# Attention and a gated convolution on one core: the w_val weights, xh and xl at other SBUF offsets, and another order of the work

## The chip, the cores and the metric

The kernel runs on one core of a Trainium2 chip. TensorE (PE in the profile, its weight loads PEld), VectorE (DVE), ScalarE (ACT), GpSimd (POOL) and SyncE (SP) each work through their own list of instructions in order and wait for one another by semaphores. SP does no arithmetic here; it issues every DMA. The metric is the time of one execution on the device, in microseconds.

## What is computed

The reference, cut to its core (`log`, `exp` and so on are numpy's):

```python
# q, k, v: (4, 8, 768, 64)
k_sum = k.reshape(B, H, nb, 32, D).max(axis=3)
v_sum = v.reshape(B, H, nb, 32, D).mean(axis=3)
scores_l = where(abs(pos_i - pos_j) < 16, scale * q @ k.T, -1e9)
scores_s = scale * q @ k_sum.T + log(32)
a = softmax(concatenate([scores_l, scores_s]))       # eps 1e-9
x = (a @ concatenate([v, v_sum])).to (4, 768, 512)
gate = sigmoid(causal depthwise convolution of x with conv_w, 5 taps)
out = (gate * (x @ w_val)) @ w_out                   # w_val, w_out: 512 x 512
```

## The kernel before

The work falls into 12 groups g (4 batches times 3 thirds of the sequence, 256 positions each); a group has two units u of four heads. A unit is computed in two halves r of two heads each. Every piece of work has a short name, and the string `ORDER` is a list of these names; a loop at the end of the kernel calls them one after the other. Each engine (and SP's list of DMAs) receives its instructions in exactly this order; nothing reorders them later, and semaphores make consumers wait. The pieces that matter here, with the lines of the kernel before:

- `s` scores on TensorE (L515), `n` the mask and row maximum on VectorE (L531), `e` exp on ScalarE (L544), `r` reciprocal of the row sum on VectorE (L551), `m` normalisation of p on GpSimd (L556), `t` transposes of p on TensorE (L566), `c` their copy to `pts` (L573), `x` the product with v on TensorE (L583).
- `X`, `Y` copies of the product to `xh` (rounded to fp32r) and `xf` (full fp32) on ScalarE (L594, L598), `Z` the rest `xl` = xf - xh on GpSimd (L602), `I`, `T`, `G` the gate: start value, taps on VectorE (L620), tanh.
- `v` the product with w_val on TensorE (L640). `v g.cp.r` makes 12 matmuls that accumulate one 128x256 tile: eight with `xh` as the moving operand (with the high part and the low part of the weights by turns, for four chunks of 128 rows), then four with `xl` and the high part. The stationary operand is a 128x128 block of the tile `wv`. There are 44 such pieces in fp32r, 528 matmuls; group 0 does it in fp32 with the tile `wf` instead.
- `gf`, `gh`, `gl` the gated value, its rounded part and the rest; `o` the product with w_out on TensorE (L676), 12 matmuls of 512 columns with `gh` or `gl` stationary and `wo` moving; `ob` and `O` scale and store.
- `Lk`, `Lq`, `Lv`, `Lu`, `Lwv`, `Lwo` loads; `Lu b.i` fetches a batch's transposed values (tile `vT`) for the block means that `tv` sums on GpSimd (L248, four halvings and a last sum), `vsp` transposes on TensorE and `vsc` copies out; `F g` writes these means into the value tile by four DMAs (L325). `ks` and `kc` make the block maxima of the keys, `vp`, `vc`, `vb`, `vbc` the means of batch 0, `W` warm-up matmuls on zeros, `hal` the convolution's halo.

Tiles lie in SBUF in the order in which the pools are opened, and within a pool in the order of first use. In the kernel before the small constants (pool `csm`: mask, taps, lag, row sums) come first and fill 2432 bytes of a partition from 16512, so that `ident`, `wv`, `wo`, `wf`, `pts`, `gh`, `gl`, `xh` and `xl` all start at a multiple of 512 bytes.

Of the kernel before, what the change touches and what calls it, by code (L numbers as in the profile page):

```python
# [60 lines left out]
r2 n3.1 x0.1 t1.0 Lk1.0 m1.1 Lwv2 ks1.1 I0 Y0 c1.0 T0.0 s4.0 e3.0 s4.1 t1.1 c1.1 x1.0 e3.1 rbwv0
wlwv3 m2.1 m2.0 n4.1 shwv0 n4.0 ks1.0 r3 orwv0 x1.1 t2.1 c2.1 Y1 shwv2 rbwv2 s5.0 s5.1 orwv2
t2.0 T0.1 n5.1 Lv1 Lu1.1 Lk1.3 Lq3 tv1.2 e4.0 m3.0 c2.0 kc1.1 kc1.0 m3.1 Lu1.0 wcwv2 hal1 v0.0.0
F1 e4.1 wcwv1 G0 v0.0.1 t3.1 v0.1.0 n5.0 c3.1 t3.0 Lk1.2 s6.0 s6.1 I1 r4 ks1.3 x2.0 wcwv0 c3.0
e5.0 x2.1 Y2 T1.0 n6.1 ks1.2 n6.0 gf0.0 wlwv2 tv1.1 m4.0 t4.0 v0.1.1 tv1.0 X2 x3.0 c4.0 x3.1
kc1.3 kc1.2 Lwo1 Lu1.3 s7.0 tv1.3 rbwo1 e5.1 m4.1 s7.1 Z2 vsp1 t4.1 X3 Y3 Z3 wlwv0 v1.1.0 T1.1
# [46 lines left out]
def tile_attention_then_gated_conv(  # L113
# [204 lines left out]
    def fill_vs(g):  # L318
# [470 lines left out]
```

## Time and profile before

| | |
|---|---|
| median of 3 runs | 243.63 us (243.48 to 244.19) |
| profiled execution, its own time | 242.4 us |
| its span (first to last instruction) | 239.8 us |
| PE / ACT / DVE / POOL busy, share of the span | 95 / 79 / 76 / 63 % |
[...]

The profiled execution's time is 2.6 us longer than its span (what lies before the first and after the last instruction), and 1.2 us (0.5%) under the median. A matmul's busy time overlaps with that of the next, so the distance between the starts of matmuls, not their durations, tells what they cost.

### The profile page before, as it was taken

How to read it: one execution, taken by the hardware profiler on the slowest of the kernel's cores; microseconds unless marked ns; L12 is line 12 of the kernel's file. 1: busy time of each engine (PE TensorE's matmuls, PEld its weight loads, DVE VectorE, ACT ScalarE, POOL GpSimd, SP SyncE). 2: the span in 40 equal slices, each digit the busy share in tenths (PEclk: the TensorE clock that was granted, in tenths of full speed). 3: DMA queues.
4: the chain of work that ended last, by engine and by line, in shares of the span. 5: the costliest groups of instructions: out<-in, count | busy, mean ns of one | idle time of the engine just before them, and what ended most of it. 6: DMA issues, size and time to landing. Idle time of an engine off the chain costs nothing.

```text
span 239.8 us, 7492 instructions
## 1 busy us (share of the span) xinstructions
PE 227.1 (95%) x2736; PEld 197.6 (82%) x2736; DVE 182.8 (76%) x698; ACT 190.6 (79%) x620; POOL 151.0 (63%) x222
## 2 busy tenths in 40 slices
PE   4778999999999999999989999999999999999993
PEld 1347788899998899898888898898988998899982
DVE  4899999998899979978989689868586565435800
ACT  2589999989999987998997999997896398174322
POOL 4153998971999989678678809994069603822620
PEclk9999999999999999999999999999999999999999
DMA  6999989999388468600693777405506221120022
GB/s 208 378 404 405 405 323 310 391 321 354 72 264 302 147 220 283 228 31 6 189 406 95 256 210 247 160 3 112 187 14 240 62 63 46 44 116 18 0 87 89
DMA packets 19812, 46.14 MB, mean 192 GB/s; under 512 B 2336, under 2 KB 7200, under 8 KB 19776
## 3 DMA queue, kind: packets, MB, share of 16 engines
q1 hardware_dynamic: 19776, 45.68, 55.5%
q8 instruction: 21, 0.34, 0.6%
q14 instruction: 15, 0.12, 0.2%
HBM read 37.21 MB, written 6.29 MB: 181 GB/s over the span
## 4 chain that ended last, share of the span: by engine, by line
PE 68%; DMA 7%; DVE 7%; POOL 6%; ACT 5%; SPq 3%; issue 2%; ACTq 0%; POOLq 0%; DVEq 0%
PE out L676 26%; PE val L640 21%; PE x L583 8%; PE pt L566 7%; PE s L515 6%; DMA k<-in_kT_dram 3%; DMA vT<-in_vT_dram 2%; DMA out_dram<-ob 2%; DVE sn L531 2%; ACT p L544 2%; POOL vT L248 2%; DVE g L620 2%; POOL p L556 2%; POOL xl L602 2%; SPq L325 1%
## 5 line engine op out<-in xcount | busy, mean ns | idle before, releaser
L620 DVE SCALAR_TENSOR_TENSOR g<-xf,cwt,g 128x256 f32<-128x256 f32 x192 | 93.7, 488 | 23.7 <-ACT xf L598 9.1
L544 ACT ACTIVATE p<-sn,nm 128x120 f32<-128x120 f32 x192 | 73.4, 390 | 7.5 <-DVE nm L531 7.5
L556 POOL TENSOR_TENSOR p<-p,ri 128x480 f32<-128x480 f32 x48 | 47.0, 993 | 13.8 <-DVE ri L552 9.8
L640 PE MATMUL val<-xh,wv 128*128 128x256 f32 x352 | 51.9, 290 | 0.0
L640 PEld LDWEIGHTS val<-xh,wv 128*128 128x128 f32 x352 | 44.9, 190 | 0.2
L531 DVE CUSTOM_DVE_ANT_0 sn<-s,mask 128x120 f32<-128x120 f32 x192 | 41.7, 276 | 4.1 <-PE s L515 3.9
L676 PE MATMUL out<-wo,gh 128*128 128x512 f32 (+1 forms) x184 | 44.3, 383 | 0.0
L602 POOL TENSOR_TENSOR xl<-xf,xh 128x512 fp32r<-128x512 f32 x22 | 28.2, 1289 | 25.2 <-ACT xh L594 16.9
L654 POOL TENSOR_TENSOR gl<-gf,gh 128x512 fp32r<-128x512 f32 x22 | 28.1, 1287 | 22.7 <-ACT gh L651 22.7
L676 PEld LDWEIGHTS out<-wo,gh 128*128 128x128 f32 x184 | 32.9, 188 | 6.2 <-issue 0.2
L544 ACT ACTIVATION_READ_ACCUMULATOR p<-sn,nm 128x1 f32 x192 | 37.3, 194 | 0.0
L573 ACT COPY pts<-pt 120x512 f32<-120x512 f32 x48 | 28.0, 583 | 11.6 <-PE pt L566 11.5
L566 PE MATMUL pt<-ident,p 128*120 128x128 f32 x192 | 30.1, 279 | 1.9 <-POOL p L556 1.7
L583 PE MATMUL x<-pts,v 120*64 120x64 f32 x768 | 29.8, 226 | 0.1
L583 PEld LDWEIGHTS x<-pts,v 120*64 120x64 f32 x768 | 26.1, 137 | 4.1 <-issue 1.3
L640 PE MATMUL val<-xl,wv 128*128 128x256 f32 x176 | 28.7, 284 | 0.6 <-POOL xl L602 0.6
L515 PE MATMUL s<-k,q 64*64 64x120 f32 x768 | 26.1, 272 | 2.2 <-POOL xf L456 0.6
L248 POOL TENSOR_TENSOR vT<-vT 128x384 f32<-128x384 f32 (+3 forms) x44 | 25.0, 568 | 5.0 <-DMA vT<-in_vT_dram 2.4
L566 PEld LDWEIGHTS pt<-ident,p 128*120 128x120 f32 x192 | 21.2, 137 | 7.1 <-POOL p L556 2.3
L515 PEld LDWEIGHTS s<-k,q 64*64 64x64 f32 x768 | 20.1, 134 | 7.5 <-POOL k L234 2.2
L640 PEld LDWEIGHTS val<-xl,wv 128*128 128x128 f32 x176 | 24.3, 191 | 1.0 <-POOL xl L602 1.0
L676 PE MATMUL out<-wo,gl 128*128 128x512 f32 (+1 forms) x92 | 23.8, 380 | 0.0
(64 smaller groups left out, 273.1 us busy)
## 6 DMA issues: line engine op xcount, KB each, us to landing
v<-in_vw_dram SPq DMA_DIRECT2D x24, 512.0 KB
k<-in_kT_dram SPq DMA_DIRECT2D x16, 478.0 KB
vT<-in_vT_dram SPq DMA_DIRECT2D x16, 384.0 KB
out_dram<-ob SPq DMA_DIRECT2D x23, 256.0 KB
q<-in_qT_dram SPq DMA_DIRECT2D x11, 512.0 KB
raw_wv<-in_wv_dram SPq DMA_DIRECT2D x4, 512.0 KB
raw_wo<-in_wo_dram SPq DMA_DIRECT2D x4, 512.0 KB
v<-vs SPq DMA_DIRECT2D x36, 48.0 KB
```

What stands on the lines that cost most here:

```text
L248: nc.gpsimd.tensor_tensor(dst, src[:, :, :n], src[:, :, n : 2 * n], ALU.add)
L515: nc.tensor.matmul(sp(u)[64 * e : 64 * e + 64, h, c * KW : c * KW + KW], qt(g)[64 * h : 64 * h + 64, pr, i * QT : i * QT + QT], ktile[b, p ...
L531: nc.vector.tensor_tensor_reduce(sn(u)[:, n, :], sp(u)[:, h, c * KW : c * KW + KW], mask[:, mv, :], -1.0 / math.sqrt(D), 3.0e38, ALU.add, ...
L544: nc.scalar.activation(pr_(u)[:, n, :], sn(u)[:, n, :], AF.Exp, bias=nm(u)[:, n : n + 1], scale=-1.0, accum_out=rs(u)[:, n, 0:1],)
L556: nc.gpsimd.tensor_tensor(pr_(u)[:, w], pr_(u)[:, w], st["ri", u][:, w].unsqueeze(2).broadcast_to([P, TPU, KW]), ALU.mult,)
L566: nc.tensor.transpose(pt[:KW, i, :], pr_(u)[:, TPU * r + i, :], ident)
L583: nc.tensor.matmul(dst, v[:KW, i, c0 : c0 + D], src, start=True, stop=g > 0)
L602: nc.gpsimd.tensor_tensor(xl(g)[:, two(hp), :], xf(g)[:, two(hp), HALO:], xh(g)[:, two(hp), :].bitcast(F32), ALU.subtract,)
L620: nc.vector.scalar_tensor_tensor(gp(u)[:, r], xf(g)[:, pr, o : o + SG], cwt[:, pr, o : o + 1], gp(u)[:, r], ALU.mult, ALU.add,)
L640: nc.tensor.matmul(pp[:, r], w, x, start=(n == 0), stop=(n == len(terms) - 1))
L654: nc.gpsimd.tensor_tensor(gl(g)[:, two(cp), :], grp["gf", g, cp], gh(g)[:, two(cp), :].bitcast(F32), ALU.subtract)
L676: nc.tensor.matmul(pp, x, w, start=(n == 0), stop=(n == len(terms) - 1))
```

## The change

**The layout.** `wv` gets a pool of its own that is opened first, then come small tiles (`ks`, `nm`, `ri`, together 448 bytes), then `xh` and `xl` (pool `px`; the raw w_out words that share their buffers move with them), then small tiles again (`vsT` and one row sum, 448 bytes), then everything else; the constants come last. The starts of the tiles modulo 512 bytes, worked out from the sizes of the tiles:

| tile | before | after |
|---|---|---|
| wv (stationary in `v`) | 0 | 128 |
| xh, xl (moving in `v`) | 0 | 64 |
| wo, gh, gl, wf, gf, ident, pts, v, q | 0 | 0 |
| p, three buffers | 64, 320, 64 | 256, 0, 256 |
| xf, two buffers | 320, 384 | 0, 64 |

All blocks of `wv`, `xh` and `xl` that a matmul reads lie at multiples of 512 bytes from the tile's start, so every one of the 528 matmuls has its operands at these offsets. No instruction is added or removed, and no buffer count changes.

**The order.** `ORDER` is another permutation of the same words; every engine gets the same instructions in another sequence. Two of its lines stand in the diff. Three places:

On TensorE before the first product with v (`x_0`): `pt` are transposes, `vb` those of batch 0's block means, the number after `s`, `x`, `p` is the unit, the two numbers after `pt` unit and half. Before:

```order
L301 MATMUL vb_1_344<-ident_91,vpad_94 128x128 x4
L301 MATMUL vb_0_349<-ident_91,vpad_94 128x128 x4
L295 LDWEIGHTS warm_95
L295 MATMUL warm_out_116<-warm_95 128x512
L295 LDWEIGHTS warm_95
L295 MATMUL warm_out_116<-warm_95 128x512
L515 MATMUL s_3_356<-k_0_2_134,q_1_247 64x120 x8
L515 MATMUL s_3_356<-k_0_3_187,q_1_247 64x120 x8
L583 MATMUL x_0_385<-pts_0_301,v_0_310 64x64
```

and after:

```order
L575 MATMUL pt_0_1_320<-ident_103,p_0_202 120x128 x4
L575 MATMUL pt_1_0_346<-ident_103,p_1_264 120x128 x4
L524 MATMUL s_3_352<-k_0_2_129,q_1_198 64x120 x8
L524 MATMUL s_3_352<-k_0_3_175,q_1_198 64x120 x8
L299 LDWEIGHTS warm_107
L299 MATMUL warm_out_125<-warm_107 128x512
L305 MATMUL vb_1_398<-ident_103,vpad_106 128x128 x4
L305 MATMUL vb_0_405<-ident_103,vpad_106 128x128 x4
L299 LDWEIGHTS warm_107
L299 MATMUL warm_out_125<-warm_107 128x512
L592 MATMUL x_0_431<-pts_0_311,v_0_313 64x64
```

The transposes of unit 1 and the scores of unit 3 now stand ahead of `vb`; before, the scores stood behind it and the first transposes of unit 1 behind `x_0`.

On SP in the middle of the program, where the means of batch 2 (`vs_2`) are written into the value tile of group 6 (`F6`) and the values of batch 3 (`vT_3_...`) are fetched. Before:

```order
L204 DMA vT_3_1_1838<-in_vT_dram 128x768
L691 DMA out_0_dram<-ob_2_1_1766 128x512
L211 DMA v_6_1933<-in_vw_dram 128x1024 x2
L325 DMA v_6_1933<-vs_2_2012 12x2x512 x4
L195 DMA q_8_2071<-in_qT_dram 128x1024
L691 DMA out_0_dram<-ob_1_0_1662 128x512
L204 DMA vT_3_3_2074<-in_vT_dram 128x768
L211 DMA v_7_2082<-in_vw_dram 128x1024 x2
L199 DMA k_3_0_2207<-in_kT_dram 128x956
```

and after:

```order
L199 DMA q_7_1761<-in_qT_dram 128x1024
L208 DMA vT_3_3_1780<-in_vT_dram 128x768
L329 DMA v_5_1581<-vs_1_960 12x2x512 x4
L199 DMA q_8_1832<-in_qT_dram 128x1024
L700 DMA out_0_dram<-ob_2_0_1601 128x512
L203 DMA k_3_2_1835<-in_kT_dram 128x956
L215 DMA v_6_1967<-in_vw_dram 128x1024 x2
L329 DMA v_6_1967<-vs_2_1897 12x2x512 x4
L208 DMA vT_3_0_2189<-in_vT_dram 128x768
L208 DMA vT_3_2_2191<-in_vT_dram 128x768
L700 DMA out_0_dram<-ob_3_0_2180 128x512
```

The load of `vT_3_3` stood behind the four DMAs that wait for `vs_2`; now it stands ahead of them, and those of `vT_3_0` and `vT_3_2` follow them.

On GpSimd between the two halves of unit 10's normalisation (`p_10`; `vT_2_1` and `vT_2_3` are values of batch 2 that `tv` sums, `k_2_...` the block maxima that `kc` writes). Before, from the first half to the second:

```order
L556 TENSOR_TENSOR p_10_1437<-p_10_1437,ri_10_1528 128x480
L248 TENSOR_TENSOR vT_2_1_1325<-vT_2_1_1325 128x24x16
L248 TENSOR_TENSOR vT_2_1_1325<-vT_2_1_1325 128x24x8
L248 TENSOR_TENSOR vT_2_1_1325<-vT_2_1_1325 128x24x4
L248 TENSOR_TENSOR vT_2_1_1325<-vT_2_1_1325 128x24x2
L248 TENSOR_TENSOR vsT_2_1_1597<-vT_2_1_1325 128x24
L234 COPY k_2_2_950<-ks_2_2_1684 128x7x12
L234 COPY k_2_2_950<-ks_2_2_1684 128x6x12
L602 TENSOR_TENSOR xl_4_1751<-xf_4_1544,xh_4_1682 128x512
L234 COPY k_2_3_1515<-ks_2_3_1699 128x7x12
L234 COPY k_2_3_1515<-ks_2_3_1699 128x6x12
L556 TENSOR_TENSOR p_10_1437<-p_10_1437,ri_10_1528 128x480
```

and after, where the first half stands five rows ahead, from the last sum of `vT_2_1` to the second half:

```order
L252 TENSOR_TENSOR vsT_2_1_1698<-vT_2_1_1549 128x24
L463 TENSOR_SCALAR xf_4_1645<-xf_3_1293 128x4x4
L252 TENSOR_TENSOR vT_2_3_1543<-vT_2_3_1543 128x24x16
L252 TENSOR_TENSOR vT_2_3_1543<-vT_2_3_1543 128x24x8
L252 TENSOR_TENSOR vT_2_3_1543<-vT_2_3_1543 128x24x4
L252 TENSOR_TENSOR vT_2_3_1543<-vT_2_3_1543 128x24x2
L252 TENSOR_TENSOR vsT_2_3_1748<-vT_2_3_1543 128x24
L238 COPY k_2_3_1477<-ks_2_3_1692 128x7x12
L238 COPY k_2_3_1477<-ks_2_3_1692 128x6x12
L238 COPY k_2_2_788<-ks_2_2_1613 128x7x12
L238 COPY k_2_2_788<-ks_2_2_1613 128x6x12
L565 TENSOR_TENSOR p_10_1359<-p_10_1359,ri_10_1538 128x480
```

One sum of a value tile, two pairs of copies and one `xl` stood between the two halves; now it is two sums, a halo and two pairs of copies, and both halves of `xl_4` follow behind.

## Rows read from the trace of the kernel before

**Rows 1.** The page: the span, busy times and slices of the whole execution.

```profile
span 239.8 us, 7492 instructions
...
PE 227.1 (95%) x2736; PEld 197.6 (82%) x2736; DVE 182.8 (76%) x698; ACT 190.6 (79%) x620; POOL 151.0 (63%) x222
...
PEclk9999999999999999999999999999999999999999
```

**Rows 2.** Busy time of each engine from 20 to 180 us, columns as headed.

```profile
core 0: us, PE busy (x) PEld busy (x) DVE busy (x) ACT busy (x) POOL busy (x), PEclk, DMA share, GB/s
...
20.00:180.00 160.00, 157.62 (x2146) 140.61 (x2146) 140.34 (x558) 148.57 (x502) 119.16 (x166) 1.00 0.65 218
```

**Rows 3.** The chain that ended last, pieces in time: start us, us, what.

```profile
55.63 7.15 PE out L676 x64
...
158.70 1.43 PE val L640 x12
```

**Rows 4.** Groups of instructions by line, TensorE: busy us, mean ns.

```profile
L640 PE MATMUL val<-xh,wv 128*128 128x256 f32 x352 | 51.9, 290 | 0.0
...
L640 PE MATMUL val<-xl,wv 128*128 128x256 f32 x176 | 28.7, 284 | 0.6 <-POOL xl L602 0.6
```

**Rows 5.** TensorE's timeline, single starts: start us, us, operation.

```profile
194.24 0.52 PE L640 MATMUL val<-xh,wv 128*128 128x256 f32 x3
194.36 0.52 PE L640 MATMUL val<-xh,wv 128*128 128x256 f32 x3
194.49 0.52 PE L640 MATMUL val<-xh,wv 128*128 128x256 f32 x3
...
229.91 0.52 PE L676 MATMUL out<-wo,gh 128*128 128x256 f32 x3
230.02 0.52 PE L676 MATMUL out<-wo,gh 128*128 128x256 f32 x3
```

**Rows 6.** Lines 566 and 620: duration ns min/median/max, first and last start.

```profile
L566 PE MATMUL pt<-ident,p x192: 270/273/326, 14.7 to 211.5; 128*120 128x128 f32 x192
...
L620 DVE SCALAR_TENSOR_TENSOR g<-xf,cwt,g x192: 437/490/494, 24.7 to 225.9; 128x256 f32<-128x256 f32 x192
```

**Rows 7.** Timelines of VectorE and TensorE in the first 21 us, and busy times there.

```profile
4.55 0.95 DVE L220 TENSOR_REDUCE ks<-k 128x24 f32<-128x768 f32 x1
...
18.50 1.09 PE L301 MATMUL vb<-ident,vpad 128*128 128x128 f32 x8 [0.36 <-POOL vpad L284]
...
20.94 0.34 PE L583 MATMUL x<-pts,v 120*64 120x64 f32 x4
...
4.55:18.25 13.70, 11.02 (x124) 5.29 (x122) 12.14 (x56) 8.62 (x43) 4.93 (x22) 1.00 1.03 388
```

**Rows 8.** The chain that ended last, 111 to 127 us.

```profile
111.61 0.59 ACT vs L315
...
116.59 5.71 DMA vT<-in_vT_dram
...
125.19 0.95 POOL p L556
```

**Rows 9.** GpSimd's and TensorE's timeline at unit 10, and TensorE's at 126 us.

```profile
87.49 2.49 POOL L248 TENSOR_TENSOR vT<-vT 128x384 f32<-128x384 f32 x4 [0.94 <-DMA vT<-in_vT_dram]
...
90.24 0.99 POOL L556 TENSOR_TENSOR p<-p,ri 128x480 f32<-128x480 f32 x1
...
94.34 1.29 POOL L602 TENSOR_TENSOR xl<-xf,xh 128x512 fp32r<-128x512 f32 x1
...
95.97 1.93 POOL L556 TENSOR_TENSOR p<-p,ri 128x480 f32<-128x480 f32 x2
...
94.63 0.60 PE L566 MATMUL pt<-ident,p 128*120 128x128 f32 x4
...
98.66 0.65 PE L566 MATMUL pt<-ident,p 128*120 128x128 f32 x4
...
126.19 0.65 PE L566 MATMUL pt<-ident,p 128*120 128x128 f32 x4 [0.89 <-POOL p L556]
```

More of the change, by code (lines that the diff above doesn't have):

```diff
@@ L61 @@
[L61 to L66, printed above, removed]
@@ new lines @@
+s0.0 n0.0 kc0.1 Lk0.3 Lp2 Ln1 W11 s0.1 W12 Lp3 ks0.2 vp3.0 n0.1 Lq1 W13 W14 e0.0 ks0.3 kc0.2 W15
+ez kc0.3 vc3.0 s1.0 W16 e0.1 Ln0 Lc n1.0 W17 s1.1 Lwv3 Ln2 vp1.0 r0 n1.1 e1.0 e1.1 Lwv0 vp1.1
+vp0.0 shc m0.0 hal0 s2.0 t0.0 s2.1 W18 W19 m0.1 r1 vc1.0 m1.0 c0.0 Lv0 rbwv3 Lwv2 t0.1 vp0.1
+n2.1 n2.0 vp2.0 c0.1 vp2.1 rbc e2.0 t1.0 m1.1 s3.0 vc0.0 vc2.0 c1.0 Lwv1 rbwv0 s3.1 vp3.1 vc0.1
+vc2.1 vc1.1 n3.1 vc3.1 shwv3 W20 shwv0 orwv0 orwv3 n3.0 orc vb1 vbc1 vb0 Lu1.1 Lq2 Lv1 vbc0
+Lk1.0 Lk1.1 e2.1 wcwv3 rbwv2 W21 x0.0 x0.1 W22 W23 t1.1 Y0 I0 r2 shwv2 c1.1 wcwv0 orwv2 x1.0
@@ new lines @@
+x1.1 shwv1 rbwv1 s4.0 wcwv2 Y1 s4.1 T0.0 e3.0 orwv1 e3.1 wlwv3 m2.1 m2.0 v0.0.0 t2.0 wlwv0
+v0.0.1 n4.1 T0.1 ks1.0 r3 ks1.1 n4.0 wlwv2 Lu1.2 c2.0 G0 Lk1.2 tv1.1 m3.1 m3.0 t2.1 wcwv1 I1 F1
+v0.1.0 c2.1 T1.0 t3.1 s5.0 s5.1 Lwo1 n5.1 tv1.2 x2.0 e4.0 Lk1.3 c3.1 x2.1 Lq3 e4.1 t3.0 v0.1.1
+kc1.1 kc1.0 n5.0 Lu1.0 Lu1.3 Lv2 Y2 X2 c3.0 x3.0 e5.0 r4 x3.1 m4.1 s6.0 m4.0 t4.0 X3 Lwo3 Lwo0
+T1.1 gf0.0 Y3 s6.1 Lk2.2 F2 Lwo2 Z2 ks1.3 ks1.2 n6.0 Z3 hal1 e5.1 c4.0 G1 r5 wlwv1 kc1.3 m5.0
+tv1.0 v1.1.0 hal2 kc1.2 tv1.3 v1.0.0 gf0.1 n6.1 I2 v1.1.1 t4.1 T2.0 v1.0.1 e6.0 rbwo1 c4.1 T2.1
@@ new lines @@
+t5.0 vsp1 m5.1 s7.0 shwo0 s7.1 x4.0 e6.1 rbwo0 vsc1 x4.1 c5.0 orwo0 G2 gf1.0 t5.1 I3 o0.0.0
+o0.1.0 shwo1 orwo1 X4 Y4 wcwo0 rbwo2 rbwo3 o0.0.1 o0.1.1 x5.0 c5.1 shwo2 n7.0 n7.1 shwo3 Lq4
+e7.0 x5.1 s8.0 s8.1 orwo3 orwo2 e7.1 wcwo3 X5 gh1.0 r6 n8.0 n8.1 Lv3 o0.0.2 o0.1.2 o0.1.3 m6.0
+Z4 m6.1 o0.0.3 Lu2.2 Y5 s9.0 Z5 s9.1 T3.0 r7 T3.1 t6.0 Lk3.3 F3 ob0.1 Lv4 e8.0 ob0.0 c6.0 wcwo2
+G3 gl1.0 Lq6 Lq5 v2.1.0 n9.1 Lk2.1 I4 wcwo1 t6.1 v2.1.1 v2.0.0 wlwo0 m7.1 m7.0 c6.1 t7.1 n9.0
+x6.0 wlwo1 wlwo3 wlwo2 x6.1 s10.0 gf1.1 T4.0 T4.1 s10.1 hal3 gh1.1 gl1.1 Lk2.0 O0.0 Lu2.0 tv2.2
@@ new lines @@
+e8.1 c7.1 t7.0 r8 n10.0 e9.0 G4 v2.0.1 m8.0 O0.1 F4 m8.1 I5 gf2.0 e10.0 e9.1 X6 o1.0 o1.1 Y6
+c7.0 T5.0 T5.1 t8.1 n10.1 s11.0 tv2.0 G5 I6 s11.1 x7.0 r9 x7.1 gf2.1 ks2.1 c8.1 gh2.0 t8.0 ks2.0
+Lk2.3 T6.0 gh2.1 c8.0 T6.1 n11.1 gl2.0 X7 ob1.0 n11.0 gl2.1 o2.0 o2.1 Y7 e10.1 ob1.1 r10 G6
+Lu2.3 I7 m9.0 Lu2.1 O1.0 kc2.1 Z7 Z6 kc2.0 m9.1 m10.1 t9.0 v3.1.0 ob2.1 Lv5 O1.1 Lk3.1 x8.0
+e11.0 ob2.0 c9.0 x8.1 ks2.2 T7.0 T7.1 s12.0 s12.1 t9.1 Y8 e11.1 c9.1 G7 X8 I8 v3.0.0 v3.1.1 r11
+n12.0 ks2.3 n12.1 tv2.1 t10.1 gf3.1 c10.1 e12.0 v3.0.1 x9.0 x9.1 hal4 tv2.3 kc2.3 kc2.2 m10.0
@@ new lines @@
+Lk3.0 Lq7 gf3.0 T8.0 Y9 X9 s13.0 Lu3.3 s13.1 Z8 t10.0 vsp2 e12.1 T8.1 n13.0 r12 n13.1 c10.0
+gh3.0 gh3.1 Z9 F5 Lq8 O2.0 Lk3.2 v4.0.0 G8 I9 m11.0 v4.1.0 T9.0 t11.0 v4.1.1 e13.0 c11.0 vsc2
+gl3.1 m11.1 T9.1 x10.0 e13.1 x10.1 hal5 m12.0 gl3.0 s14.0 s14.1 t11.1 o3.0 c11.1 Lv6 F6 G9 Y10
+X10 I10 tv3.3 m12.1 t12.0 n14.0 n14.1 r13 gf4.1 s15.0 s15.1 x11.0 x11.1 m13.1 c12.0 T10.0 t12.1
+v4.0.1 T10.1 ks3.0 e14.0 Y11 X11 gh4.1 e14.1 gf4.0 c12.1 G10 r14 n15.0 Z11 o3.1 t13.1 kc3.0 Z10
+m13.0 m14.1 gl4.1 m14.0 hal6 I11 v5.1.0 x12.0 x12.1 n15.1 s16.0 e15.0 ob3.0 c13.1 e15.1 Y12
@@ new lines @@
+Lu3.0 Lu3.2 O3.0 s16.1 t13.0 v5.1.1 v5.0.0 tv3.2 T11.0 T11.1 X12 c13.0 G11 I12 t14.1 v5.0.1 r15
+x13.0 x13.1 ks3.1 n16.0 n16.1 gf5.1 Lv7 T12.0 s17.0 gh4.0 e16.0 c14.1 gl4.0 s17.1 t14.0 X13 Y13
+ob3.1 e16.1 o4.0 F7 Z13 m15.0 c14.0 m15.1 kc3.1 o4.1 T12.1 n17.0 G12 r16 n17.1 ks3.2 ks3.3 gf5.0
+I13 e17.0 Lq9 O2.1 T13.0 e17.1 s18.0 ob4.0 s18.1 m16.1 hal7 kc3.3 Z12 x14.0 m16.0 T13.1 x14.1
+t15.0 v6.0.0 c15.0 t15.1 Lu3.1 v6.1.0 c15.1 Y14 X14 t16.1 O4.0 O3.1 Lv8 n18.1 r17 n18.0 v6.0.1
+Z14 kc3.2 G13 I14 T14.0 x15.0 x15.1 gh5.0 ob4.1 gh5.1 c16.1 s19.0 s19.1 t16.0 T14.1 gf6.0 n19.1
@@ new lines @@
+v6.1.1 X15 e18.0 Y15 m17.1 gl5.1 gl5.0 G14 e18.1 I15 o5.1 o5.0 n19.0 gf6.1 r18 T15.0 c16.0 hal8
+F8 tv3.0 m17.0 e19.0 t17.0 O4.1 Lv9 Lq10 m18.1 Z15 v7.1.0 ob5.1 e19.1 x16.0 x16.1 c17.0 T15.1
+s20.0 s20.1 m18.0 hal9 tv3.1 gh6.0 t17.1 gh6.1 v7.1.1 G15 Y16 c17.1 X16 I16 n20.0 t18.0 v7.0.0
+n20.1 r19 gf7.1 x17.0 x17.1 O5.1 Lq11 T16.0 s21.0 s21.1 T16.1 c18.0 vsp3 t18.1 gh7.1 Lv10 ob5.0
+e20.0 X17 vsc3 e20.1 G16 I17 Y17 c18.1 v7.0.1 n21.0 n21.1 r20 T17.0 Z16 m19.1 gl7.1 gl6.0 gl6.1
+o6.1 o6.0 s22.0 O5.0 F9 e21.0 s22.1 x18.0 x18.1 m19.0 ob6.1 Z17 F10 t19.0 m20.0 ob6.0 e21.1
@@ new lines @@
+T17.1 G17 c19.0 I18 X18 n22.0 gf7.0 v8.1.0 n22.1 Y18 t19.1 v8.1.1 c19.1 x19.0 x19.1 s23.0 s23.1
+t20.0 T18.0 gh7.0 e22.0 v8.0.0 gf8.1 c20.0 T18.1 n23.0 r21 n23.1 gl7.0 Lv11 e22.1 X19 G18 I19
+gh8.1 Y19 O6.0 o7.0 F11 o7.1 m20.1 Z18 t20.1 O6.1 c20.1 v8.0.1 T19.0 x20.0 gl8.1 m21.0 Z19 gf8.0
+e23.0 x20.1 t21.0 ob7.1 c21.0 gh8.0 Y20 ob7.0 r22 T19.1 v9.0.0 hal10 m21.1 m22.1 t22.1 v9.1.0
+gl8.0 m22.0 c22.1 G19 I20 X20 t21.1 c21.1 v9.1.1 T20.0 gf9.1 T20.1 x21.0 x21.1 t22.0 v9.0.1 Y21
+e23.1 G20 r23 m23.1 gh9.1 o8.0 o8.1 I21 O7.1 O7.0 X21 c22.0 x22.0 x22.1 ob8.1 T21.0 m23.0 Z21
@@ L109 @@
+hal11 Z20 t23.0 v10.1.0 gf9.0 T21.1 X22 gh9.0 c23.0 ob8.0 v10.0.0 t23.1 v10.1.1 G21 Y22 I22
+c23.1 x23.0 gf10.1 gh10.1 x23.1 gl9.0 gl10.1 gl9.1 v10.0.1 T22.0 gf10.0 O8.0 O8.1 T22.1 o9.1
+o9.0 G22 ob9.1 gh10.0 Y23 X23 gl10.0 Z23 I23 ob9.0 o10.1 Z22 T23.0 T23.1 v11.0.0 v11.1.0 v11.1.1
+v11.0.1 G23 O9.1 gf11.1 gf11.0 O9.0 gh11.1 gl11.1 ob10.1 gh11.0 gl11.0 o10.0 o11.0.1 o11.1
+ob10.0 O10.0 O10.1 ob11.0.1 ob11.1 o11.0.0 O11.0.1 O11.1 ob11.0.0 O11.0.0
 """
@@ L128, in tile_attention_then_gated_conv @@
     P = 128
-    csm = ctx.enter_context(tc.tile_pool(name="csm", bufs=1))
+    pwv = ctx.enter_context(tc.tile_pool(name="pwv", bufs=1))
+    tiny = ctx.enter_context(tc.tile_pool(name="tiny", bufs=2))
+    px = ctx.enter_context(tc.tile_pool(name="px", bufs=2))
+    tiny2 = ctx.enter_context(tc.tile_pool(name="tiny2", bufs=1))
     cpool = ctx.enter_context(tc.tile_pool(name="cpool", bufs=1))
@@ L216, in key_max @@
     def key_max(b, pr):
-        ks = sm.tile([P, NB], F32, tag="ks", name=f"ks_{b}_{pr}", bufs=BUFS["ks"])
+        ks = tiny.tile([P, NB], F32, tag="ks", name=f"ks_{b}_{pr}", bufs=BUFS["ks"])
         own = ktile[b, pr][:, OFF_O : OFF_O + STEP * NT]
@@ L239, in prep_v @@
     def prep_v(b, pr):
-        t = sm.tile([P, NB], F32, tag="vsT", name=f"vsT_{b}_{pr}", bufs=BUFS["vsT"])
+        t = tiny2.tile([P, NB], F32, tag="vsT", name=f"vsT_{b}_{pr}", bufs=BUFS["vsT"])
         src = vTt.pop((b, pr)).rearrange("p (n c) -> p n c", c=BLK)
@@ L330, in tile_attention_then_gated_conv @@
     wsplit = {
-        nm: cpool.tile([P, 4, 2, DM], F32R, tag=nm, name=nm) for nm in ("wv", "wo")
+        nm: p.tile([P, 4, 2, DM], F32R, tag=nm, name=nm) for nm, p in (("wv", pwv), ("wo", cpool))
     }
@@ L369, in load_w @@
         tag = RAW_TAG[nm][k]
-        raw = wk.tile(
+        raw = (px if tag[0] == "x" else wk).tile(
             [P, 2 * DM if wide else DM], U32, tag=tag, name=f"raw_{nm}{k}", bufs=BUFS[tag]
@@ L431, in part @@
         if key not in grp:
-            grp[key] = (sm if kind == "xf" else wk).tile(shape, dt, tag=kind, name=f"{kind}_{g}", bufs=BUFS[kind])
+            home = {"xf": sm, "xh": px, "xl": px}.get(kind, wk)
+            grp[key] = home.tile(shape, dt, tag=kind, name=f"{kind}_{g}", bufs=BUFS[kind])
         return grp[key]
@@ L466, in attn @@
         if key not in st:
-            st[key] = (sm if kind in ("nm", "p") else wk).tile(shape, F32, tag=kind, name=f"{kind}_{u}", bufs=BUFS[kind])
+            home = {"nm": tiny, "p": sm}.get(kind, wk)
+            st[key] = home.tile(shape, F32, tag=kind, name=f"{kind}_{u}", bufs=BUFS[kind])
         return st[key]
@@ L477, in nm @@
         return attn("nm", u, [P, NP])
-    sums = [csm.tile([P, NP, 2], F32, tag=f"rs{i}", name=f"rs{i}") for i in range(4)]
+    sums = [
+        (csm if i else tiny2).tile([P, NP, 2], F32, tag=f"rs{i}", name=f"rs{i}")
+        for i in range(4)
+    ]
     def rs(u):
@@ L549, in recip @@
     def recip(u):
-        ri = st["ri", u] = sm.tile([P, NP], F32, tag="ri", name=f"ri_{u}", bufs=4)
+        ri = st["ri", u] = tiny.tile([P, NP], F32, tag="ri", name=f"ri_{u}", bufs=4)
         nc.vector.tensor_reduce(ri, rs(u), AX.X, ALU.add)
```

50 lines of the change are left out of this document (2 added, 48 removed).

## Prediction

> **What bounds the kernel now.** [...] From 20 to 180 us TensorE is busy for 157.6 of 160 us, ScalarE for 148.6, VectorE for 140.3 and GpSimd for 119.2 [rows 2]: after the start TensorE loses some 2.4 us in 160. So the time is made of what TensorE's matmuls cost from start to start, plus some 20 us of start, plus a few waits. ScalarE has 11 us of room in that stretch, enough for what is at stake here.
>
> The chain that ended last gives those distances, since it runs along TensorE and counts each piece until the next starts. A `val` piece of 12 matmuls with 256 columns takes 1.43 us, 0.1192 us each [rows 3]. The 64 fp32 matmuls of group 0's output, each with a new block of 128 weight columns as in `val`, take 7.15 us, 0.1117 us each [rows 3]. So a weight load per matmul does not need 0.1192 us; something adds up to 7.5 ns to each `val` matmul. Single starts show that this is no constant: inside one `val` group two neighbours lie 0.12 and 0.13 us apart, and the first fp32r matmul of 256 columns after a run of 512-column ones only 0.11 us ahead of the second [rows 5]. Same shapes, operands at multiples of 512 bytes in all of them, and a pace that depends on how the weight load and the stream of the moving operand lie in time. I read this as the two reads hindering each other now and then; where, no row says.
>
> **The change, part by part.** *The offsets of wv, xh and xl.* There are 352 + 176 = 528 such matmuls [rows 4]. All now have the weights at 128 and the moving operand at 64 modulo 512 bytes. The trace has no fp32r matmul whose two operands start at different offsets, so the price is bounded from both sides. Below: 0.1117 us, where the weight load alone would set the pace, gives 528 x 7.5 ns = 4.0 us. Above: if every one went like the worst neighbours, 0.13 us, it would cost 528 x 10.8 ns = 5.7 us. Nothing in the rows excludes a loss. The nearest row is the fp32r matmul of the same shape at 0.11 us; since it stands alone, and steady runs settle at 0.12, I take the middle between 0.1117 and 0.1192, 0.1155 us: 528 x 3.75 ns = 2.0 us gained, all of it on the path, since from 20 us on TensorE hardly waits [rows 2].
>
> [...]
>
> *Offsets of p, xf and the small tiles.* Priced at nothing: the slices of p that the transposes load already lie 480 bytes apart, at 16 different offsets, and the transposes' durations (270 and 273 ns, lowest and median) do not spread with them; the taps read xf at many offsets and stay at 490 ns in the median, 494 at most [rows 6]. If they did move by 1%, VectorE's taps would change by 0.9 us in all, hidden behind TensorE, since VectorE idles for 20 us of the 160 [rows 2].
>
> *The order at the start.* TensorE's unbroken work begins with `x_0` at 20.94 us, behind `vb` at 18.50, which waited for the block means [rows 7]. VectorE makes these, and from 4.55 us, where the first key maximum starts, to 18.25 us it is busy for 12.14 of 13.70 us [rows 7]: another order can save 1.6 us of its idle time at most. The new one puts one more piece of `n` and a reciprocal ahead of the last block means, which takes part of that back. TensorE also gets the first four transposes of unit 1 done ahead of `x_0` that otherwise stood behind it, at the 0.11 us of the fp32 matmuls above 0.4 us of work. I take this 0.4 us as the gain in all; the bounds are 1.6 gained and as much lost, should the keys, now fetched first, delay the values.
>
> *The loads of batch 3.* Before, the chain goes from the copy of batch 2's means at 111.61 through SP's four DMAs into the value tile to the load of `vT_3_3`, which is issued behind them, starts at 116.59 and takes 5.71 us; GpSimd waits for it in front of the normalisation of unit 15 (125.19), and TensorE's transposes idle for 0.89 us [rows 8, 9]. Now this load stands ahead of the four DMAs. What GpSimd sums in front of unit 15 is then `vT_3_2`, issued two places behind the four; but between the copy of the means and this sum lie, in the order, four `val` pieces of TensorE (5.7 us at 1.43 [rows 3]), two of `out`, six of scores, six products with v and five of transposes, far more than the four DMAs and a load of 5.71 us. The stall should go: 0.9 us gained, or nothing if another load is late.
>
> *GpSimd at unit 10.* Before, the first half of p_10 ends at 91.23 (90.24 + 0.99) and the second starts at 95.97, 4.74 us later, with one sum of 2.75 us (87.49 to 90.24 is one) and one `xl` of 1.29 between them; TensorE wants the halves at 94.63 and 98.66, 4.03 us apart, and has the first 3.40 us after its end [rows 9]. Now a second sum and a halo (0.2) come in and the `xl` moves behind: 4.74 + 2.75 + 0.2 - 1.29 + 0.99 = 7.39 us from the end of the first half to the end of the second. With the old lead of 3.40 us TensorE wants it after 3.40 + 4.03 = 7.43, just in time. But both `xl_4` follow, 2.58 us, and TensorE reaches the `val` matmuls that read them after eight transposes (0.11 each) and eight matmuls (0.12), 1.84 us: 7.39 + 2.58 - 7.43 - 1.84 = 0.7 us of wait. I take 0.6; nothing if the lead is larger, 4.2 if there is none.
>
> *The sum*: -2.0 - 0.4 - 0.9 + 0.6 = -2.7 us. The profiled execution took 242.4 us (239.8 of span and 2.6 around it), which makes 239.7; the median stands 1.2 us above it, so 240.9 us.
>
> **The rivals.** *The weight load sets the pace* (0.1117 us): 4.0 for 2.0, so 238.9 us. The 0.11 us neighbours speak for it, that steady runs never keep that pace against it. Chance 0.13.
>
> *The offsets change nothing* and only the order counts: 243.63 - 0.7 = 242.9 us. For it: 0.1192 may be what fp32r costs in a steady run, whatever the addresses. Against it: the pace varies within a run. [...] Chance 0.20.
>
> *The offsets are worse.* If the two reads hinder each other at times that depend on where they start, another start can as well make them meet oftener. If the steady pace were half way to the worst neighbours, 0.1246 us, that is 528 x 5.4 ns = 2.9 us lost, 243.63 + 2.9 - 0.7 = 245.8. It decides from 0.1192 + 0.7/528, 0.1205 us. Chance 0.13.
>
> *GpSimd is late* at unit 10 or at another place of that kind, without the lead it had: +4.2 in place of 0.6 gives 244.5 us. Against it: GpSimd is idle for 41 us of the 160 [rows 2]. It decides from a lead of 0.7 us and less. Chance 0.12.
>
> **How the numbers follow.** The forecast (a gain of 1 to 3 us in `val`, the other terms within 0.7 us of mine) has 0.42, and 240.9 us. 0.3% of 243.63 is 0.73 us, about what a measurement of this kernel can tell from no change: faster is under 242.9, slower over 244.4. Faster: 0.40 of the forecast, 0.13, half of the 0.20, 0.03 of the late GpSimd, 0.66. Slower: 0.12 of the worse offsets, 0.05 of GpSimd, 0.03 of the unchanged offsets, 0.20. The same: 0.14. The range reaches from 238.2 (the weight-load pace with the stall gone and none new) to 245.0: above it lie most of the worse offsets and little else, below it the best of the start on top of the best offsets, together no more than 0.2. The forecast alone: 239.6 to 242.2.
>
> **What would show it.** A `val` piece of 12 in the chain at about 1.39 us for 1.43 (1.34 at the weight-load pace, 1.43 where offsets do nothing, 1.50 where they harm), with `out` at the old distances. `x_0` at about 20.5 us. No wait of TensorE for unit 15's p; a wait of about 0.6 us for `xl_4`. Wrong would be above all the pace: each nanosecond there is 0.53 us. Also wrong if TensorE, once faster, waits for ScalarE between 20 and 180 us: then its busy share there falls below 157.6 of 160 while the pace improves.

## The result, and the profile after

The changed kernel takes 241.11 us (median of 4, 240.09 to 242.27), the kernel before 243.71 beside it (243.48 to 244.19): ratio 0.9894, 95% interval 0.9853 to 0.9935, 2.6 us or 1.1% faster. The forecast was 240.9. Timed again later (run 5), the ratio was 0.9901 (0.9867 to 0.9935).

One thing is needed to read the profile after: two of its four executions took 240.1 and 240.3 us at a granted TensorE clock of 1.00 of full speed in the mean, two 242.0 and 242.3 at 0.993. The profiled one is of the second kind (241.96 us, span 240.3), while that of before lay 1.3 us under its median of 243.71; so its span is 0.5 us longer than before's although the kernel is faster.

The page of the profile after: span, busy times, granted clock in 40 slices.

```profile
span 240.3 us, 7477 instructions
...
PE 225.4 (94%) x2732; PEld 197.4 (82%) x2736; DVE 184.3 (77%) x698; ACT 190.7 (79%) x620; POOL 151.6 (63%) x222
...
PEclk9999999999999999899999999999999999999999
```

Busy time by stretch in the kernel after (columns as headed):

```profile
core 0: us, PE busy (x) PEld busy (x) DVE busy (x) ACT busy (x) POOL busy (x), PEclk, DMA share, GB/s
20.00:180.00 160.00, 154.60 (x2074) 138.48 (x2075) 139.46 (x547) 146.34 (x492) 116.27 (x163) 0.99 0.64 218
...
90.00:95.00 5.00, 2.41 (x66) 2.14 (x62) 2.86 (x6) 2.86 (x12) 4.53 (x10) 1.00 1.02 407
95.00:100.00 5.00, 5.00 (x32) 5.00 (x32) 3.33 (x20) 3.62 (x13) 2.19 (x8) 0.66 0.43 141
```

From 20 to 180 us TensorE now stands idle for 5.4 of 160 us, where it was 2.4 [rows 2]. One place holds 2.6 of it, near 92 us, and behind it the granted clock is 0.66 in the mean of 5 us and 0.50 from 96 to 98 us. The chain that ended last shows what stands there, and the new pace elsewhere (start us, us, what):

```profile
72.47 1.38 PE val L649 x12
73.86 5.47 PE out L685 x24
...
86.51 6.61 DMA out_dram<-ob
93.14 0.60 ACT ob L694
93.74 0.48 ACT pts L582
94.36 0.62 PE pt L575 x4
94.98 4.38 PE val L649 x24
...
104.25 2.74 PE val L649 x24
...
121.86 1.42 PE val L649 x12
...
228.65 8.35 PE out L685 x48
237.03 0.38 ACT ob L694
```

A `val` piece of 12 takes 1.38 us, some 1.41 or 1.42, where they took 1.43, a few 1.42 [rows 3]; 24 `out` matmuls take 5.47, as before. The 24 `val` matmuls right behind the wait take 4.38 us instead of 2.74. The rows just ahead of the wait say why it is there: a store of 256 KB, issued at 86.51, takes 6.61 us; ScalarE needs its `ob` buffer and waits, and the copy of the transposes to `pts`, for which TensorE waits, is queued behind. The timeline has the two issues on SP, the wait on ScalarE, and five places on TensorE (in brackets the idle time before the row and what ended it):

```profile
84.48 0.91 SPq L215 DMA_DIRECT2D v<-in_vw_dram  x2
86.51 0.34 SPq L700 DMA_DIRECT2D out_dram<-ob  x1
...
93.14 0.60 ACT L694 ACTIVATE ob<-out 128x512 f32<-128x512 f32 x1 [2.14 <-DMA out_dram<-ob]
...
94.33 0.41 PEld L575 LDWEIGHTS pt<-ident,p 128*120 128x120 f32 x4 [2.79 <-POOL vT L252]
94.36 0.62 PE L575 MATMUL pt<-ident,p 128*120 128x128 f32 x4 [2.59 <-ACT pts L582]
...
20.59 0.33 PE L592 MATMUL x<-pts,v 120*64 120x64 f32 x2
21.20 0.27 PE L594 MATMUL x<-pts,vb 120*64 120x64 f32 x1 [0.29 <-ACT vb L309]
...
25.08 0.34 PE L592 MATMUL x<-pts,v 120*64 120x64 f32 x4 [0.82 <-ACT g L623]
...
35.66 0.62 PE L575 MATMUL pt<-ident,p 128*120 128x128 f32 x4 [1.19 <-ACT pts L582]
...
125.27 0.65 PE L575 MATMUL pt<-ident,p 128*120 128x128 f32 x4
```

The last row has no bracket: the 0.89 us at unit 15 [rows 9] are gone. `x_0` starts at 20.59 (20.94 before [rows 7]), but TensorE then waits at 21.20, 25.08 and 35.66. The two releasers at 94 us disagree: the weight load's column names GpSimd's sums, the matmul's ScalarE's copy. Run 3 below decides.

### The profile page after: what moved, and what is told of

The parts are those of the page before. It is cut to its first block, busy times and chain, and to the rows that moved or that the text cites. A ratio compares the mean times of both kernels' runs of the same rounds, so it can differ in the third digit from the quotient of the medians.

```text
span 240.3 us, 7477 instructions
## 1 busy us (share of the span) xinstructions
PE 225.4 (94%) x2732; PEld 197.4 (82%) x2736; DVE 184.3 (77%) x698; ACT 190.7 (79%) x620; POOL 151.6 (63%) x222
## 4 chain that ended last, share of the span: by engine, by line
PE 80%; ACT 7%; DMA 5%; DVE 4%; SPq 1%; issue 1%
PE val L649 27%; PE out L685 26%; PE x L592 10%; PE pt L575 9%; PE s L524 8%; DMA out_dram<-ob 3%; DMA q<-in_qT_dram 3%; ACT p L553 2%; DVE g L629 2%; ACT pts L582 2%; DVE sn L540 1%; ACT ob L694 1%; SPq L203 1%; ACT g L623 1%; PE vsp L315 1%
## 5 line engine op out<-in xcount | busy, mean ns | idle before, releaser
L565 POOL TENSOR_TENSOR p<-p,ri 128x480 f32<-128x480 f32 x48 | 47.6, 1002 | 16.5 <-DVE ri L561 16.5
L649 PEld LDWEIGHTS val<-xh,wv 128*128 128x128 f32 x352 | 45.4, 194 | 0.3 <-issue 0.2
L649 PE MATMUL val<-xl,wv 128*128 128x256 f32 x176 | 27.9, 282 | 0.0
L655 DVE SCALAR_TENSOR_TENSOR gf<-gt,val 128x512 f32<-128x512 f32 x24 | 16.3, 680 | 11.7 <-PE val L649 11.7
```

What stands on the lines that cost most here:

```text
L565: nc.gpsimd.tensor_tensor(pr_(u)[:, w], pr_(u)[:, w], st["ri", u][:, w].unsqueeze(2).broadcast_to([P, TPU, KW]), ALU.mult,)
L649: nc.tensor.matmul(pp[:, r], w, x, start=(n == 0), stop=(n == len(terms) - 1))
```

## The experiments

Ratios are against the kernel before, timed beside each run. Runs 1 to 4 share one chip, runs 5 to 10 another.

**1. The layout alone.** The order of before in the changed kernel:

```
- ORDER = """ Lk0.0 Lk0.1 Mu Lp0 wz W0 ...   (after)
+ ORDER = """ Lk0.0 Mi cv Mu wz Lp0 ...      (before)
```

> The kernel before with the order of before and the SBUF layout of the changed kernel (w_val weights at 128, xh and xl at 64 modulo 512 bytes). If the offsets set the pace of the `val` matmuls, a piece of 12 takes 1.38 us in the chain as in the changed kernel, `out` stays at 2.72 to 2.75, and the time is that of before less 528 x 3.6 ns = 1.9 us: about 241.8 us. If the pace comes from the order (what runs ahead of each piece), the pieces stay at 1.43 and the time at 243.7 us.

Measured: 242.42 us (before 244.22), ratio 0.9921 (0.9887 to 0.9956), 1.9 us gained (1.1 to 2.8). Its chain, and TensorE's timeline at unit 15:

```profile
127.53 1.38 PE val L649 x12
```

```profile
126.88 0.65 PE L575 MATMUL pt<-ident,p 128*120 128x128 f32 x4 [1.17 <-POOL p L565]
```

The offsets alone bring the pace: all 42 pieces without a wait inside go at under 118 ns from start to start, of before's none. The old stall at unit 15 grew from 0.89 to 1.17 us in this profile, which fits a faster TensorE that reaches it sooner.

**2. The order alone.** The changed kernel's order in the kernel before.

> The order of the changed kernel with the layout of before. If the offsets set the pace, `val` pieces are back at 1.43 us, and the time stands 1.9 us above that of the changed kernel: about 243.0 us, or less if TensorE's wait near 92 us, which the changed kernel has, shrinks because TensorE reaches the place later. If the order sets the pace: 1.38 us a piece and about 241.1 us.

Measured: 244.35 us over all its executions (before 244.22), ratio 0.9956 (0.9913 to 1.0000), executions at a clock of 1.00 at 241.2 to 241.7 us, all others at 0.993 or less and 243.3 to 247.4. Over all its executions, then, the order alone gains nothing, and the interval of its ratio reaches 1. Its chain:

```profile
86.79 6.39 DMA out_dram<-ob
...
94.42 0.62 PE pt L566 x4
95.05 4.37 PE val L640 x24
...
117.58 1.43 PE val L640 x12
```

The pace is the old one (118.6 to 120.0 ns from start to start in all 42 pieces at the full clock), and the wait near 92 us with the lower clock behind it is there with the old layout too: it belongs to the order.

**3. The store ahead of the loads.**

```
- ... ob2.1 Lv5 O1.1 Lk3.1 ...
+ ... ob2.1 O1.1 Lv5 Lk3.1 ...
```

> The changed kernel with one word of its order moved: the store of group 1's second output block is issued on SP ahead of the two loads of v_5 (1 MB) in place of behind them. Theory: the 2.6 us for which TensorE stands still near 92 us come from ScalarE, which waits for that store to give its `ob` buffer back while the copy of p's transposes is queued behind it; the store takes 6.6 us because the loads stand ahead of it. Then the store lands some 2.6 us earlier, TensorE's wait shrinks to under 0.5 us, the clock is granted in full throughout (the wait is what it fell after), and the median falls by 2.6 us, to 4.2 where the clock had fallen: to 237 to 238.5 us. Rival: the wait belongs to GpSimd's two sums ahead of p_10, which the releaser column of the weight loads names; then nothing changes, 241.1 us.

Measured: 239.84 us (before 244.22), ratio 0.9812 (0.9760 to 0.9865): 2 us less than the changed kernel's ratio gives, though the two intervals just touch. The forecast of 237 to 238.5 us was not reached. ScalarE and TensorE in its timeline:

```profile
90.97 0.60 ACT L694 ACTIVATE ob<-out 128x512 f32<-128x512 f32 x1 [1.13 <-DMA out_dram<-ob]
92.97 0.58 ACT L694 ACTIVATE ob<-out 128x512 f32<-128x512 f32 x1
...
94.17 0.62 PE L575 MATMUL pt<-ident,p 128*120 128x128 f32 x4 [0.50 <-POOL vT L252]
```

The second `ob` no longer waits, TensorE's wait is 0.50 us for 2.59, with GpSimd's two sums where they were. The wait was the store's, behind 1 MB of loads; GpSimd's name in the weight load's column was not the cause. But the clock was not granted in full throughout, as expected: in this profile it was 0.91 in the mean from 12 to 16 us and 0.67 from 16 to 20 instead.

**4. A table of offsets.** TensorE alone:

```
+ for ow in offsets:            # 0, 64, ..., 448
+     for ox in offsets:
+         for n in range(2):
+             val_piece(pps[n], ow, ox)   # 8 x (high, low) + 4 terms, 256 columns
+         marks(1)
```

> Computes nothing of the reference: TensorE alone, with constant data and no other engine at work. For each of 8 x 8 pairs of offsets modulo 512 bytes (weights and moving operand, multiples of 64) it issues two pieces of 12 matmuls shaped as in `val`, then for each of 8 x 8 pairs one piece of 12 shaped as in `out` (512 columns). If the two reads of TensorE hinder each other by their addresses, the rows of the table differ: 0.119 us a matmul where both start at 0, about 0.115 at weights 128 and moving 64, and the table shows whether the difference of the two offsets counts or each by itself, and whether other pairs are better, 0.112 at best. If the offsets matter only beside the traffic of other engines, all 64 pairs go at one pace. [...]

The chain, for weights at 0 and the moving operand at 0, 64, 128, 192:

```profile
16.60 2.86 PE pp L104 x24
...
19.70 2.82 PE pp L104 x24
...
22.75 2.84 PE pp L104 x24
...
25.82 2.74 PE pp L104 x24
```

Mean distance in ns from one weight load to the next (from the third of a pair's row on), worked out from their starts; the rows for weights at 256 to 448 repeat these within 0.4 ns in `val` and 0.6 in `out`:

```
val: weights \ moving   0      64     128    192    256    320    384    448
  0                    119.4  117.8  118.5  113.9  119.7  117.8  118.5  113.9
 64                    117.8  119.9  117.9  118.3  117.9  119.9  117.9  118.3
128                    118.3  117.8  119.8  117.7  118.4  113.9  119.6  117.8
192                    117.9  118.7  117.8  119.8  117.8  120.0  113.6  119.3
out: moving \ stationary
  0                    229.9  233.4  232.4  229.8  229.1  233.4  232.3  229.9
 64                    229.9  231.9  232.9  232.3  228.9  232.0  232.9  232.4
128                    231.9  230.0  229.4  233.4  232.4  229.8  229.0  233.4
192                    232.9  232.9  230.4  232.0  232.9  232.2  230.4  232.0
```

With nothing else at work the pace depends on the pair. Operands at one offset modulo 256 are among the worst (119.3 to 119.9 ns); most others go at 117.7 to 118.7, a few at 113.6 to 113.9. Differing modulo 256 is not enough: 192 and 320 go at 120.0. For 128 and 64, the changed kernel's pair, about 115 was expected; the table has 117.8. In `out` the equal pair 0 and 0, where the kernel has its operands, is near the best.

**5 to 7. The changed kernel again, another good pair, an equal pair.** In 6 only `xh` and `xl` move, to 320, in 7 to 128; small tiles change sides:

```
6: - home = {"nm": tiny, "p": sm}    + home = {"nm": tiny2, "p": sm}   (and ri likewise)
7: - (csm if i else tiny2).tile(     + (csm if i else tiny).tile(
```

> The changed kernel unchanged, timed on the same chip beside the next three. Ratio to the kernel before about 0.989; the executions fall into two groups some 2 us apart, those with a granted clock of 0.99 and those with 1.00, if the clock falls after TensorE's wait near 92 us in some executions and not in others.

> The changed kernel with xh and xl at 320 in place of 64 modulo 512 bytes (weights still at 128; no other tile moves, the order is the same). By the table of pairs, 128 and 320 go at 113.9 ns a matmul where 128 and 64 go at 117.8 and 0 and 0 at 119.4. If the pace of a pair in the table carries over, pieces of 12 take 1.37 us and less, all of them, the mean distance is 0.114 in place of 0.116 us, and the time falls by 528 x 2 ns = 1.1 us against the changed kernel: about 240.0 us. If the real kernel's pace is set by the work around each piece, it stays at 0.116 and 241.1 us.

> The changed kernel with xh and xl at 128 in place of 64: both operands at the same offset, which is not 0. If the difference of the two offsets counts, the pace is that of before (0.1196 us a matmul, pieces of 1.43) and the time 528 x 3.6 ns = 1.9 us over the changed kernel, about 243.0 us. If it is enough that the tiles do not start at a multiple of 512, pieces stay at 1.38 and the time at 241.1 us.

Measured (before 243.73): the changed kernel 242.00 us, ratio 0.9901 (0.9867 to 0.9935); 320 in place of 64: 241.55, 0.9872 (0.9814 to 0.9931), not to be told from it; 128: 243.68, 0.9984 (0.9949 to 1.0018), the gain gone. A piece at 128 and 128, then one at 128 and 320:

```profile
144.74 1.43 PE val L649 x12
```

```profile
142.74 1.38 PE val L649 x12
```

So equal offsets cost the old pace at 128 as at 0 (118.6 to 120.0 ns in all 44 pieces), and leaving 512 does nothing by itself. But the table's 113.9 for 128 and 320 against 117.8 for 128 and 64 did not carry over: expected 240.0 us, not found. The starts tell more: in the profile after, of 42 pieces at the full clock 23 go at 113.3 to 114.5 ns from their fourth to their twelfth matmul, 18 at 117.6 to 117.9, one between, 115.4 in the mean. (Before, all are at 118.6 to 120.0, but for two with a wait for `xl` inside.) At 128 and 320 they go at the same two paces, 26 pieces at the faster one, 115.1 in the mean. Both new pairs have two steady paces, and a piece falls into one of them. Which one goes with the place in the order and not with the pair: of the last 32 of the 44 pieces, 30 have the same pace in all six profiles with the new order and one of the two pairs, while with the order of before (run 1) other pieces have it. What in the order decides is open.

Of after's 12 executions on this chip those at a clock of 1.00 took 239.3 to 241.9 us, those at 0.992 to 0.993 240.7 to 243.6: two groups that overlap, where two some 2 us apart were expected.

**8. The best of it.** The pair of 6 with three places of the order changed:

```
- m9.0 Lu2.1 O1.0 kc2.1 ... Lv5 O1.1       + m9.0 O1.0 Lu2.1 kc2.1 ... O1.1 Lv5
- T0.1 ks1.0 r3 ks1.1                      + r3 T0.1 ks1.0 ks1.1
- c2.0 G0 ... t2.1 wcwv1 I1 F1 v0.1.0 c2.1 + c2.0 ... t2.1 c2.1 G0 wcwv1 I1 F1 v0.1.0
```

> The better pair (xh and xl at 320) with three places of the order changed: both stores of group 1's second half stand ahead of the loads of vT_2_1 and v_5; the reciprocal of unit 3 ahead of three pieces of VectorE; the copy of unit 2's second transposes ahead of the tanh of unit 0 on ScalarE. Theory: TensorE's wait near 92 us and its 1.2 us at 35 us go (the clock then has no long wait to fall after) and the pace is 0.114: from the 239.8 us of the run with one store moved, less 1.1 for the pair, 0.5 for the rest of the wait and about 1.0 for the start, 237.2 us. Rival: the later order takes the start's gain back (VectorE and ScalarE are busy for 97% there), which leaves 238.2 us; a load that now comes late shows as a wait of TensorE for vT or v.

Measured: 238.46 us (before 243.73), ratio 0.9773 (0.9720 to 0.9825), the lowest median of all versions and 3.5 us under the changed kernel on the same chip; its interval overlaps that of run 3. The forecast was 237.2, the rival 238.2: the 1.1 us for the pair did not come (run 6), and at the start TensorE still waits 0.98 us, now for VectorE's row maximum (37.83 us), where it waited 1.19. Its chain has no wait near 92 us:

```profile
92.07 0.98 PE s L522 x32
93.06 0.58 PE pt L573 x4
93.64 2.83 PE val L647 x24
```

**9. TensorE busy through the wait.** The scores of unit 12 three times over, the store as late as ever. If the clock fell to 0.50 behind the wait because TensorE stood still, it should now stay at 1.00 there, and the 1.6 us by which the 24 `val` matmuls took longer in the profile after (4.38 us for 2.74) should be gained, or in part, since the clock does not fall in every execution. If it falls for another reason, the time stays the same:

```
- s12.0 s12.1 t9.1
+ s12.0 s12.1 s12.0 s12.1 s12.0 s12.1 t9.1
```

> The changed kernel with the scores of unit 12 computed three times in a row in place of once (the same numbers into the same tile; 64 more matmuls, 2.0 us), just ahead of the place near 92 us where TensorE waits 2.6 us for ScalarE. The wait itself stays as it is, since ScalarE gets its buffer back no sooner; only TensorE is busy through most of it. [...]

Measured: 241.77 us (before 243.90), ratio 0.9894 (0.9852 to 0.9936), the same as the changed kernel; of a gain of up to 1.6 us nothing shows, though each ratio is known to 1 us only. Its chain at the place, and the granted clock on its page:

```profile
95.31 0.60 ACT ob L692
...
96.52 0.62 PE pt L573 x4
97.15 2.74 PE val L647 x24
```

```profile
PEclk9899999999999999999999999999999999999999
```

ScalarE's wait is as it was; TensorE's is 0.88 us for 2.59, and the clock stayed at 1.00 behind it (2.74 us for 4.38). But in this execution it had fallen near 10 us instead (0.71 in the mean from 8 to 12 us, 0.86 from 12 to 16), and four of its six executions were at or under 0.993, as against 8 of 12 of the changed kernel in run 5. So this run does not settle what the clock follows.

**10. The load alone.** In the kernel before:

```
- F6 Lq8 O1.0 Lu3.3
+ Lu3.3 F6 Lq8 O1.0
```

> The kernel before, order and layout, with one word moved: the load of vT_3_3 is issued ahead of the four DMAs that wait for batch 2's means in place of behind them. Theory (the prediction's step on the loads of batch 3): the 0.89 us for which TensorE waits at unit 15's transposes go, and the time falls by 0.9 us, ratio about 0.9963. Rival: GpSimd is late there anyway, or another load that is now issued later takes the place; then the wait stays in part and the ratio is 1.000.

Measured: 242.07 us (before 243.90), ratio 0.9944 (0.9915 to 0.9972), 1.4 us gained (0.7 to 2.1). Unit 15's transposes follow without a wait:

```profile
127.26 0.60 PE L564 MATMUL pt<-ident,p 128*120 128x128 f32 x4
```

## Why the prediction was right, and where it was not

**The offsets: right, in size too.** Forecast 1.39 us for a piece and 2.0 us in all; measured 1.38 (some 1.42), and 1.9 us when made alone (run 1). The reading behind it, that the weight load and the moving stream hinder each other depending on where they start, fits the table: with TensorE alone the pace depends on the pair of starts. How they hinder each other no trace shows. What was wrong is the picture of an in-between pace: 0.1155 us is a mean over two paces, 113.4 and 117.8 ns. That the middle of the prediction's two bounds met this mean is luck, since no row spoke of how many pieces go at either; the rival's 0.1117 us was never reached. The runs do not agree with the rival by which the offsets change nothing: with no other engine at work the same shape and data go at 113.6 to 120.0 ns by offset alone (run 4). With the same order and nearly the same places of all other tiles, equal offsets at 128 lose the gain (run 7); so it came neither from the order nor from the tiles beside.

**Offsets of p, xf and small tiles at nothing:** nothing in the profile after speaks against it (transposes 270 ns at least and 273 in the median, taps 490 in the median, as in [rows 6]); not tried by itself.

**The start: the sign failed.** `x_0` came 0.35 us earlier, as forecast, but the step stopped there: it took the order behind `x_0` at nothing. Up to the first fp32r `val` (43.39 us after, 44.38 before) the changed order has 1.8 us less work done (four transposes, 32 score matmuls and the `vsp` transposes fewer: 0.36, 0.99 and 0.44 us from start to start before), so it is 0.8 us behind there, inside the step's bounds. The 0.82 us ahead of `x_1` and the 1.19 us at 35.66, both on ScalarE, took the gain back.

**The loads of batch 3: right.** The stall is gone, and run 10 gives 1.4 us (0.7 to 2.1) for this one word, forecast 0.9.

**GpSimd at unit 10: failed.** No wait for `xl_4` appeared, not even in run 8, where no wait near 92 us hides it (the first row holds the last half of `p_9` and the first of `p_10`):

```profile
89.43 1.93 POOL L563 TENSOR_TENSOR p<-p,ri 128x480 f32<-128x480 f32 x2
...
97.77 0.99 POOL L563 TENSOR_TENSOR p<-p,ri 128x480 f32<-128x480 f32 x1
...
100.60 1.28 POOL L609 TENSOR_TENSOR xl<-xf,xh 128x512 fp32r<-128x512 f32 x1 [0.60 <-ACT xh L601]
```

```profile
96.31 0.60 PE L573 MATMUL pt<-ident,p 128*120 128x128 f32 x4
...
102.16 0.62 PE L647 MATMUL val<-xl,wv 128*128 128x256 f32 x4
```

From the end of the first half (91.36) to that of the second (98.76) are 7.40 us, forecast 7.39. But TensorE transposes the first half at 96.31, 4.95 us after its end, where the prediction took 3.40 from the old order. This lead was the term that failed: with 1.55 us more of it no wait of 0.7 is left, and `xl_4`, though held up 0.60 us by ScalarE, ends at 101.88, 0.28 us before the matmuls that read it. Before's 0.6 us of waits for `xl` [rows 4] are gone instead. (By its own terms the step's worst case is 4.1 us and not 4.2: 7.39 + 2.58 - 4.03 - 1.84.)

**What no step had.** The wait of 2.6 us for a store's buffer and, in some executions, a stretch at a granted clock of 0.50 behind it, worth 1.6 us (4.38 - 2.74). The prediction looked at each queue's moved loads for what they delay on GpSimd and TensorE, not for the stores behind them, whose buffers ScalarE needs. Its last paragraph named the sign of it, a busy share under 157.6 while the pace improves; it is 154.6, so by that sign the prediction was wrong here, and it had no price for it. In the other direction it missed the end: from the end of the last `out` matmuls to the end of the span are 3.3 us (240.3 - 228.65 - 8.35), where before

```profile
224.60 11.09 PE out L676 x60
235.71 0.38 ACT ob L685
236.10 0.28 ACTq L784
```

leaves 4.1 us (239.8 - 224.60 - 11.09); only one copy of half a block now stands behind the last matmul.

The sum over the two profiles: -1.9 offsets, +0.8 start, -0.9 stall, -0.6 `xl`, +2.6 and +1.6 near 92 us, -0.8 end, +0.8 us, against +0.5 measured in the spans; 0.3 us in many small distances stay unresolved. From there to the -2.6 us of the medians the account does not reach: 0.9 us lie outside the spans (2.6 us before, 1.7 after), the profile of before stood 1.3 us under its median, and that of after 0.85 over its own. Why executions of before are mostly slower than its profile is seen only in part: with the same start, TensorE also waits at 52 us for the block means' DMAs in the profiles of run 10 (0.67 us) and run 1 (0.72 and 0.18), and in run 10 at 64 us behind an `ob` copy of ScalarE (0.81).

The order's share was forecast at -0.7 us. Its terms come to +2.7 in the two profiles; measured alone it was 0.9956, -1.1 us (-2.1 to 0), and nothing by the median over all executions. These do not agree, and the gap is open. So that the time came out within 0.2 us of the forecast is in good part luck: terms that were wrong by 1.2 us each (`xl`, the start) and terms that were missing (4.2 near 92 us, 0.8 at the end) did not show in it. That the offsets alone bring 1.9 us and the load 1.4 is not luck.

**Open.** What makes the clock fall. It fell behind the wait in four of five profiles that have the wait (0.66 in the mean from 95 to 100 us in the profile after; 0.70, 0.63 and 0.62 from 96 to 100 us in runs 2, 5 and 6), and at that place in none of the six that have under 1 us there. The fifth with the wait (run 7, 0.50 from 12 to 24 us), like three of those six (runs 3 and 8, 0.67 from 16 to 20 us; run 9, 0.71 from 8 to 12), had it fallen in the first 30 us instead. So each of the eight profiles with the new order has one such fall ahead of its last matmul, and none of the three with the old order has (before, runs 1 and 10); yet other executions of the new order show a clock of 1.00. TensorE standing still at the place goes with the fall there; that filling the wait changed no median (run 9) speaks against the wait as its only cause.

## What to carry to other kernels

Where TensorE is the bound and a weight load goes with each matmul, look at the distance of starts at one shape; if it varies, try stationary and moving tiles at offsets that differ modulo 256 bytes, measured first in a small table and then in the kernel, since the table's ranking among good pairs did not hold there, only that equal offsets are bad (119.3 to 119.9 ns in the table, 118.6 to 120.0 at 0 and at 128 in the kernel). The shape counts: with 512 columns the equal pair 0 and 0 was near the best (229.9 ns, the best 228.9). When an order is changed, follow each store as well as each load: here a store behind a megabyte of loads (6.61 us to its landing) kept a buffer, the buffer an engine (2.14 us), and that engine the one queued behind it (2.59 us). One word moved, the store's or the load's, was worth about as much as the whole layout (2.0 and 1.4 us against 1.9). And check a forecast by its terms: this one met the time with two terms wrong and two missing.

## What the hardware showed that was not expected

In `val` the table repeats with a period of 256 bytes in the offset of the weights, to 0.4 ns. In the moving operand it does so only for weights at 0 and 64: with weights at 128, 64 gives 117.8 and 320 gives 113.9 ns. No pair of the table reaches the 111.7 ns of group 0's fp32 output [rows 3]; the fastest take 113.6 to 113.9.

In the kernel the same piece mostly has the same one of the two paces, 113.4 or 117.8 ns, from run to run: 30 of the last 32 pieces, over the six profiles with the new order and one of the two good pairs.
